# Two more units' convolution from TensorE to the channel-major jobs, with one product of most jobs moved from GpSimd to ScalarE

## Chip, cores, metric

The kernel runs on one core of a Trainium2 chip (trn2). The metric is device microseconds of a whole execution; a profile's span is 1.75 to 2.1 us shorter than the timed run. A ratio is the mean time of one kernel's fast runs over that of the kernel before in the same rounds, so it is not quite the ratio of the medians quoted beside it.

## The reference

```python
# causal convolution of 7 taps, one softmaxed set of taps per head (8 heads of 24 channels)
out = np.einsum('hk,bskhg->bshg', w, x_unf)        # x: 8 x 4096 tokens x 192 channels
x = out.reshape(32768, 192)
g = x @ w_gate                                     # 192 -> 1536
silu = g * (1.0 / (1.0 + np.exp(-g)))
return (silu * (x @ w_val) @ w_out)                # 1536 -> 192
```

## The kernel before

The tokens are cut into 16 units of 4 blocks of 512. A block goes through 12 steps, one for each chunk of 128 hidden features: a step multiplies the convolved block with a chunk of the gate and value weights on TensorE, takes silu on ScalarE (ACT) and the product h on VectorE (DVE). The down matmuls of finished chunks stand in four slots, after chunks 1, 4, 7 and 10.

The convolution runs ahead of its use in one of two ways. For a unit that is not "pooled" it is a band-matrix multiplication on TensorE (`conv_half`, twice a unit). For a pooled unit it is six jobs on channel-major tiles (channels on the partitions, tokens along the row), each of seven products with a per-channel tap: some on ACT, two on DVE, the rest on GpSimd (POOL), which also does the additions. Three jobs serve two blocks. GpSimd issues the "cast" that fetches a unit's tokens in fp16; SyncE's queue then issues the transposes to channel-major tiles and, once jobs are done, the "placement" of a block's results where the gate and value matmuls read them.

```python
    POOLED = (2, 4, 5, 6, 8, 9, 10, 12, 13, 14, 15)
    FIRST, ON_DVE, ON_ACT, ON_POOL = 0, (1, 2), (3,), (4, 5, 6)
    ...
        def add(part, k):                       # GpSimd: two 128x512 inputs
            total = job["total"]
            seq(nc.gpsimd.tensor_tensor(
                job["dst"] if k == K - 1 else total, total, part, op=ALU.add))

        def proceed():                          # once both DVE products are issued
            if job["dve"]:
                return
            while job["parts"]:
                add(*job["parts"].pop(0))       # what ScalarE has made
            if job["act"]:
                return
            for k in ON_POOL:                   # product into "piece", then the addition
                ...
        def dve_step(k):                        # total = x * tap + total, two 128x512 inputs
            seq(nc.vector.scalar_tensor_tensor(
                job["total"], shifted(k), job["tap"][:, k : k + 1], job["total"], ...))
    ...
    def pooled_work(n, j, busy):                # after each step's slot
        if not busy:
            ...
            if j in (1, 7, 10) and ready is not None:
                dve_steps.pop(0)[1]()
            if j in (1, 7, 10) and act_steps and (ready is None or ahead < ready + 3):
                act_steps.pop(0)[1]()
    ...
        elif j % 3 == 1 and n > 18:
            k = {1: 3, 4: 4, 7: 1, 10: 2}[j]
            slot(k, b - 1 if j < 7 else b, silu[n - 2], work)   # its first load waits for silu[n - 2]
```

Slot 4 (after chunk 4) ends with the output copies of the last block, half on ACT and half on DVE. Three PSUM buffers each serve gate and value, so the gate and value matmuls of step n wait until sig and h of step n - 3 are done.

## Time and profile before

| | before |
|---|---|
| time, median of 4 runs beside the changed kernel | 779.69 us (779.4 to 779.97) |
| span of the profile | 776.2 us |
| busy share PE, DVE, ACT, POOL | 99, 87, 75, 71% |
| a unit without disturbance | 46.92 us |
| extra over 46.92 us, units 1 to 14 | 4.84 us: convolution for units 3, 7, 11 4.32, two slips 0.52 |

The start of a unit is the start of its first gate weight load in the timeline; a unit's length is the distance to the next, and whatever is over 46.92 us is TensorE time lost or spent on convolution. The lost part is called a slip. Units 0 and 15 are left out: the first holds the loads, the last the end of the program.

The second part of the page cuts the span in 40 slices and gives busy tenths; POOL rests about once in four units, where the next unit's convolution is TensorE's:

```profile
POOL 9100798899999970299999995049999999996000
```

### The profile page before, as it was taken

The numbers are of one execution on the slowest core, as the hardware profiler recorded it, in microseconds if no ns is written. First come the engines' busy times: TensorE is split into PE (matmuls) and PEld (weight loads), VectorE is DVE, ScalarE is ACT, GpSimd is POOL, SyncE is SP. The second block draws the span as 40 slices with busy tenths as digits, with TensorE's granted clock in tenths as the row PEclk, the third lists the DMA queues.
The fourth block names the chain that finished last, engine by engine and source line by source line (L and its number), as shares of the span: only waits on it lengthen the run. The fifth ranks groups of instructions, "written<-read, shape, count | busy, mean of one in ns | idle before, by whom it ended". The sixth has DMA issues, their size and how long they took to land.

```text
span 776.2 us, 27852 instructions
## 1 busy us (share of the span) xinstructions
PE 770.1 (99%) x11307; PEld 627.2 (81%) x11307; DVE 675.0 (87%) x1018; ACT 584.6 (75%) x999; POOL 551.6 (71%) x523
## 2 busy tenths in 40 slices
PE   8999999999999999999999999999999999999998
PEld 5766776788888888678888888868888888888876
DVE  7686999999999977899999987799999999997775
ACT  6676887877877766878788776678788787876664
POOL 9100798899999970299999995049999999996000
PEclk9999999999999999999999999999999999999999
DMA  9959754944532295475363158557535254221211
GB/s 138 184 117 150 163 110 107 149 101 116 111 99 70 57 191 102 121 126 114 87 129 91 38 98 157 119 138 137 92 83 124 72 108 103 69 66 40 69 57 42
DMA packets 154470, 82.37 MB, mean 106 GB/s; under 512 B 98110, under 2 KB 153798, under 8 KB 153798
## 3 DMA queue, kind: packets, MB, share of 16 engines
q1 hardware_dynamic: 136422, 64.26, 37.6%
q0 software_dynamic: 17920, 16.34, 14.7%
q8 instruction: 88, 1.44, 0.8%
q14 instruction: 40, 0.33, 0.1%
HBM read 32.68 MB, written 38.34 MB: 91 GB/s over the span
## 4 chain that ended last, share of the span: by engine, by line
PE 99%; DVE 0%; ACT 0%; issue 0%
PE val L772 36%; PE acc L798 32%; PE gate L772 28%; PE cv L476 1%; PE warm L873 1%; PE turn L445 0%; PE cv L387 0%; PE acc L819 0%; DVE h L783 0%; ACT tme L405 0%; ACT wide L345 0%; ACT sig L781 0%; ACT o_sb L961 0%; DVE o_sb L857 0%; PE taps L332 0%
## 5 line engine op out<-in xcount | busy, mean ns | idle before, releaser
L781 ACT ACTIVATE sig<-gate 128x512 f16<-128x512 f32 x768 | 458.7, 597 | 175.0 <-PE gate L772 114.5
L783 DVE TENSOR_TENSOR h<-sig,val 128x512 f16<-128x512 f16 x768 | 502.6, 686 | 91.5 <-PE gate L772 64.1
L772 PEld LDWEIGHTS <-w 64*128 64x128 f16 x4608 | 359.6, 110 | 108.8 <-issue 1.5
L772 PE MATMUL gate<-pxc,w 64*128 64x512 f16 x1584 | 370.9, 376 | 0.0
L772 PE MATMUL val<-pxc,w 64*128 64x512 f16 x1584 | 370.7, 376 | 0.1
L798 PE MATMUL acc<-wo,h 64*128 64x192 f16 x6096 | 325.6, 243 | 0.0
L798 PEld LDWEIGHTS <-h 64*128 64x128 f16 x6096 | 299.8, 94 | 27.3 <-issue 1.9
L630 POOL TENSOR_TENSOR total<-total,piece 128x512 f32<-128x512 f32 x132 | 178.5, 1353 | 11.0
L772 PE MATMUL gate<-xc,w 64*128 64x512 f16 x720 | 169.6, 376 | 0.0
L772 PE MATMUL val<-xc,w 64*128 64x512 f16 x720 | 169.6, 376 | 0.1
L645 POOL TENSOR_SCALAR piece<-x,both_taps 128x512 f32<-128x512 f16 x198 | 165.2, 834 | 0.0
L655 DVE SCALAR_TENSOR_TENSOR total<-x,both_taps,total 128x512 f32<-128x512 f16 x132 | 138.8, 1052 | 0.0
L630 POOL TENSOR_TENSOR total<-total,part 128x512 f32<-128x512 f32 x66 | 89.9, 1362 | 52.2 <-DVE total L655 50.3
L630 POOL TENSOR_TENSOR pxc<-total,piece 128x512 f16<-128x512 f32 x44 | 58.9, 1340 | 3.7
L504 POOL COPY tm<-tm 128x1280 f16<-128x1280 f16 x4 | 5.0, 1251 | 65.7 <-DVE tm L493 65.7
L680 ACT ACTIVATE part<-x,both_taps 128x512 f32<-128x512 f16 x66 | 47.1, 714 | 0.0
L680 ACT ACTIVATE total<-x,both_taps 128x512 f32<-128x512 f16 x66 | 47.1, 713 | 0.0
L857 DVE COPY o_sb<-acc 128x384 f32<-128x384 f32 x63 | 34.7, 550 | 0.0
L630 POOL TENSOR_TENSOR y<-total,piece 128x512 f16<-128x512 f32 x22 | 29.2, 1329 | 1.8
L856 ACT COPY o_sb<-acc 128x384 f32<-128x384 f32 x63 | 30.3, 480 | 0.1
L98 POOL DMA_DIRECT2D x<-in_x_dram x10 | 8.7, 885 | 24.4 <-ACT sig L781 24.4
L493 ACT CAST tm<-cv 128x480 f16<-128x480 f32 x16 | 8.2, 562 | 5.6 <-PE cv L476 5.6
(67 smaller groups left out, 85.1 us busy)
## 6 DMA issues: line engine op xcount, KB each, us to landing
out_dram<-o_sb SPq DMA_DIRECT2D x63, 384.0 KB
pxc<-pxc SPq DMA_DIRECT2D x88, 64.0 KB
pxc<-y SPq DMA_DIRECT2D x88, 64.0 KB
xs<-in_x_dram POOLq DMA_DIRECT2D x7, 768.0 KB, 6.9
x<-in_x_dram POOLq DMA_DIRECT2D x10, 480.0 KB, 9.0
scr<-tm SPq DMA_DIRECT2D x28, 130.0 KB
xs<-in_x_dram POOLq DMA_DIRECT2D x4, 774.0 KB, 7.2
x<-x SPq DMA_DIRECT2D x6, 480.0 KB
```

The costliest lines, as they stand in the source:

```text
L98: nc.gpsimd.dma_start(out=t[p0 + i0 : p0 + i1, w0 - at : w1 - at, :], in_=bass.AP(tensor=x_flat.tensor, offset=(t0 + size * w0 - pad + i0) ...
L493: eng(tm[u][:, NG * r : NG * r + NG, 2 * grp * hp : 2 * grp * hp + 2 * grp].rearrange("p g (t e) -> p g t e", t=2), banks[r][:, 0 : 2 * w] ...
L630: nc.gpsimd.tensor_tensor(job["dst"] if k == K - 1 else total, total, part, op=ALU.add)
L645: nc.gpsimd.tensor_scalar(part, shifted(k), scalar1=job["tap"][:, k : k + 1], scalar2=1.0, op0=ALU.mult, op1=ALU.mult,)
L655: nc.vector.scalar_tensor_tensor(job["total"], shifted(k), job["tap"][:, k : k + 1], job["total"], op0=ALU.mult, op1=ALU.add,)
L680: nc.scalar.activation(part, shifted(k), AF.Copy, scale=job["tap"][:, k : k + 1])
L772: nc.tensor.matmul(o, w16[m][p0 : p0 + Q, k, e::E], xc[b][k][p0 : p0 + Q, 0:TB], start=(k == 0), stop=(k == SL - 1),)
L781: silu[n] = seq(nc.scalar.activation(sg, g, AF.Silu)).ins
L783: seq(nc.vector.tensor_tensor(hj, sg, v, op=ALU.mult))
L798: nc.tensor.matmul(acc[b][bank][:, s, :], hj[p0 : p0 + Q, ts(2 * bank + s, P)], wo16[p0 : p0 + Q, j, :], start=(not second and j == 0 and ...
L856: seq(nc.scalar.copy(o_sb[:, 0:2, :], acc[b][0]))
L857: seq(nc.vector.tensor_copy(o_sb[:, 2:4, :], acc[b][1]))
```

## The change

The intent: TensorE is the bound, so take the convolution of units 7 and 11 from it. All units but 1 and 3 are then channel-major (unit 0 has its own early path). GpSimd could not do three products in every job without rests (by the means of its rows before, three jobs take it 23.7 us, and the two blocks that they serve take TensorE 23.46), so two of three jobs give one to ScalarE, which gets an extra slot after chunk 4, ahead of the output copy.

```diff
-    POOLED = (2, 4, 5, 6, 8, 9, 10, 12, 13, 14, 15)
+    POOLED = (2, *range(4, NU))
...
-    FIRST, ON_DVE, ON_ACT, ON_POOL = 0, (1, 2), (3,), (4, 5, 6)
+    FIRST, ON_DVE = 0, (1, 2)
+    SHARES = ((3, 4), (5, 6)), ((3, 4), (5, 6)), ((3,), (4, 5, 6))
...
+        on_act, on_pool = SHARES[index % len(SHARES)]
...
+            if j == 4 and act_steps and act_steps[0][0] < (
+                dve_steps[0][0] if dve_steps else n_jobs[0]
+            ) + 3:
+                act_steps.pop(0)[1]()
             k = {1: 3, 4: 4, 7: 1, 10: 2}[j]
             slot(k, b - 1 if j < 7 else b, silu[n - 2], work)
```

Cut: the uses of `on_act` and `on_pool`, and a time table for unit 3 that is not reached, since unit 3 is not in the list.

More of the change, by code (lines that the diff above doesn't have):

```diff
@@ L620, in conv_job @@
         n_jobs[0] += 1
-        job = {"dve": len(ON_DVE), "act": len(ON_ACT), "parts": []}
+        on_act, on_pool = SHARES[index % len(SHARES)]
+        job = {"dve": len(ON_DVE), "act": len(on_act), "parts": []}
         at = XP - pad
@@ L641, in proceed @@
                 return
-            for k in ON_POOL:
+            for k in on_pool:
                 part = cpool.tile([P, TB], fp32, tag="piece", name="piece", bufs=2)
@@ L686, in act_step @@
                 proceed()
-        act_steps.extend((index, lambda k=k: act_step(k)) for k in (FIRST, *ON_ACT))
+        act_steps.extend((index, lambda k=k: act_step(k)) for k in (FIRST, *on_act))
     def place(u, i):
@@ L727, in planned @@
             times = (36, 36, 36, 38, 39, 39, 41, 41, 43, 43)
+        elif v == 3:
+            cast, jobs = 60, 56
+            times = range(66, 86, 2)
         else:
@@ L741, in pooled_work @@
         step_now[0] = n
-        if not busy:
+        if not busy and j != 4:
             ready = dve_steps[0][0] if dve_steps else None
```

## The prediction

> **What bounds the kernel now.** I read the page's busy shares and its chain first, then the windows view with one window per unit (a unit is 4 blocks of 512 tokens, 48 steps), then the timeline around single steps.
>
> ```profile
> PE 770.1 (99%) x11307; PEld 627.2 (81%) x11307; DVE 675.0 (87%) x1018; ACT 584.6 (75%) x999; POOL 551.6 (71%) x523
> ...
> PE val L772 36%; PE acc L798 32%; PE gate L772 28%; PE cv L476 1%; PE warm L873 1%; PE turn L445 0%; PE cv L387 0%; PE acc L819 0%; DVE h L783 0%; ACT tme L405 0%; ACT wide L345 0%; ACT sig L781 0%; ACT o_sb L961 0%; DVE o_sb L857 0%; PE taps L332 0%
> ```
>
> The chain is TensorE from end to end: gate, value and down matmuls, and 1% of convolution (cv). The unit starts for the windows are where the first gate weight load of each 48 steps begins in the timeline; shown are units 4, 5, 6 and 7 (columns: PE, PEld, DVE, ACT, POOL busy).
>
> ```profile
> 204.16:251.08 46.92, 46.92 (x676) 41.12 (x673) 44.24 (x65) 37.82 (x64) 45.50 (x41) 1.00 0.38 95
> 251.08:298.00 46.92, 46.92 (x676) 41.13 (x673) 39.23 (x58) 32.94 (x56) 34.87 (x33) 1.00 0.57 109
> 298.00:346.35 48.35, 48.35 (x740) 36.00 (x737) 41.23 (x63) 37.17 (x64) 19.19 (x19) 1.00 0.67 127
> 346.35:393.27 46.92, 46.92 (x676) 41.21 (x673) 44.30 (x65) 37.83 (x64) 45.48 (x42) 1.00 0.48 100
> ```
>
> Every undisturbed unit takes exactly 46.92 us, at full clock, so that is TensorE's own pace (11.73 us a block). Unit 6 takes 48.35 us because the convolution of unit 7 runs on TensorE inside it (64 more matmuls). The same 48.35 stands at unit 10 (for unit 11); unit 2 (for unit 3) has 48.38. Two odd slips remain, measured the same way: units 1 and 13 take 47.17 and 47.19, 0.25 and 0.27 over.
>
> [...] The timeline agrees: gate weight loads follow one another at 215 to 216 ns while gate and val halves run side by side, and down matmuls of 192 columns every 82 ns[...]. [...] The trace agrees for the VectorE product L655: alone it takes 0.745 us; started while a GpSimd instruction has the time r left, it takes about r + 0.55 (r = 0.48 gives 1.03, r = 0.96 gives 1.51, r = 1.21 gives 1.76). [...] the trace has 0.714 for exactly the product that is added, and that is used.
>
> **The change part by part.** I built both kernels and listed which slot issues each step of the convolution jobs.
>
> *Removed from TensorE.* Units 7 and 11 get 12 channel-major jobs on ACT, DVE and POOL instead. Units 6 and 10 lose 48.35 - 46.92 = 1.43 us each: **2.86 us**. All of it lies on the path, since TensorE never rests. That row of chain, 1%, is the whole stake; unit 3 and the early blocks keep theirs.
>
> *POOL.* The jobs' rows:
>
> ```profile
> L630 POOL TENSOR_TENSOR total<-total,piece 128x512 f32<-128x512 f32 x132 | 178.5, 1353 | 11.0
> ...
> L645 POOL TENSOR_SCALAR piece<-x,both_taps 128x512 f32<-128x512 f16 x198 | 165.2, 834 | 0.0
> L655 DVE SCALAR_TENSOR_TENSOR total<-x,both_taps,total 128x512 f32<-128x512 f16 x132 | 138.8, 1052 | 0.0
> ...
> L680 ACT ACTIVATE part<-x,both_taps 128x512 f32<-128x512 f16 x66 | 47.1, 714 | 0.0
> ```
>
> A job before is 4 additions and 3 products: 4 x 1.353 + 3 x 0.834 = 7.91 us; three jobs in two blocks are 23.7 us against 2 x 11.73 = 23.46 of TensorE. So POOL could not hold that for long, which is why every fourth unit went to TensorE. After, two of three jobs lose one product (4 additions still): 7.91 + 2 x 7.08 = 22.07 us, 94% of 23.46. GpSimd keeps up, idle some 1.4 us in two blocks; one cast issue per unit (0.56 us) fits in that.
>
> *DVE.* Twelve products a unit in twelve slots, as in units 4 and 7 now: 44.3 of 46.92 us busy, unchanged in a full unit, but now in all of units 3 to 14 rather than with rests.
>
> *ACT.* Four more products a unit. Back to back it starts the next instruction 0.103 us before the last ends (median of sig to product), so 4 x (0.714 - 0.103) = 2.44 us on 37.82: 40.3 of 46.92, 86%. The average is harmless; the place is not. One block of unit 4:
>
> ```profile
> 232.83 0.48 ACT L856 COPY o_sb<-acc 128x384 f32<-128x384 f32 x1
> ...
> 233.40 1.89 ACT L781 ACTIVATE sig<-gate 128x512 f16<-128x512 f32 x3
> ...
> 234.28 1.21 PEld L798 LDWEIGHTS <-h 64*128 64x128 f16 x23
> ```
>
> The listing of waits has the first down weight load (at 234.28) wait for the sig of chunk 5, which ends at 234.00 now. With a product after sig of chunk 4 (end 232.86): product 232.76 to 233.47, output copy 233.37 to 233.85, sig of chunk 5 from 233.75 to 234.34. The one time that this load did wait in the trace (at 27.51 us) it started 0.05 us after the sig's end; so 234.39 instead of 234.28. But the load stands 0.214 us ahead of its matmul (234.50) and takes 0.094, so the matmul can still start at about 234.49. I estimate no loss in most blocks, with almost nothing to spare: 0 to 0.05 us in each of some 52 blocks, **0 to 2.6 us**; I take 0.3.
>
> *Lateness on DVE.* h of chunks 5 to 7 comes 0.35 us later. Their room, from h's end to the first weight load of the matmuls that reuse the bank, is 0.69, 0.56, 0.56 now; it stays positive.
>
> **Sum.** 779.74 - 2.86 + 0.3 = 777.2. The two slips could go (-0.5) or others come.
>
> **The rivals.** (a) *ACT blocks the down matmuls.* If copy or sig start without the 0.103 overlap after a product, sig of chunk 5 ends 0.1 to 0.2 us later, and each block loses that: 52 x 0.15 = 8 us, time about 785. For it: the margin is 0.01 us by my sum. Against it: the overlap is 0.10 wherever two ACT instructions have nothing to wait for (also CAST after CAST).
>
> (b) *Lock step of GpSimd and VectorE.* The tight place is after chunk 1: h of chunk 2 to 4 have 0.19, 0.06, 0.06 us of room, and the product of that slot stands before them. Products up to 1.505 us there cost nothing in the trace; in unit 13 one of 1.79 cost 0.27:
>
> ```profile
> 632.24 1.79 DVE L655 SCALAR_TENSOR_TENSOR total<-x,both_taps,total 128x512 f32<-128x512 f16 x1
> 633.96 1.87 DVE L783 TENSOR_TENSOR h<-sig,val 128x512 f16<-128x512 f16 x3
> ```
>
> It began 0.03 us after a GpSimd addition did. Before, GpSimd drifts against TensorE, so this is chance (2 of 45). After, GpSimd rests once in two blocks, at the job whose second product stands after chunk 7, and then always starts from the same point: the phase repeats in every period. Laying out the operations from that rest (additions 1.27, products 0.69, plus 0.44 when locked out), I find at the two slots after chunk 1 a rest of about 0.3 and 0.5 to 0.93 us of an addition, that is products of 0.9 and 1.1 to 1.48 us: no loss. If my phase is off by some 0.2 us in the bad direction, one slot in two blocks loses up to 0.27: some 24 x 0.27 = 6.5 us, time about 783.
>
> (c) *GpSimd falls behind anyway* (lockouts make it longer than 23.46): then jobs end late. They are placed 16 steps ahead of use and finish tens of steps earlier, so a lag of a few us is absorbed; only ACT's waits for part buffers could then bite. POOL at 94% speaks against it; it would give 780 to 790.
>
> (d) *The gain is hidden:* impossible to see how, as TensorE has no idle time in units 6 and 10.
>
> **Range and chances.** The floor is 779.74 - 2.86 - 0.5 = 776.4; run scatter is 0.3 on either side. (a) and (b) have no floor above it and I give them together one in five, mostly at partial size. So 776.0 to 780.2. Two per cent is 15.6 us: a gain of that is beyond the stake, a loss needs (a) and (b) in full together.
>
> **What would show it.** Right: the windows of units 6 and 10 at 46.92; no wait of down weight loads on ACT of more than 0.1 us each in the list of waits; POOL waiting for the DVE product about once in two blocks; product L655 after chunk 1 under 1.5 us; ACT's sig of chunk 5 ending about 0.34 us later. Wrong: units of 47.1 to 47.6 us all along (a: the gap stands ahead of the down loads after chunk 7; b: ahead of the gate or val matmul of chunk 5), or POOL without rests (c).

Cut from the prediction, and marked, are figures and a mechanism that no trace of this case shows; what the traces show beside them stays (where it says that a trace agrees, it is with a passage that is cut). Its sum came to 779.74 - 2.86 + 0.3 = 777.2 us, with the added ScalarE product at the traced 0.714 us. That a unit of 46.92 us could not be made shorter was the estimate; the trace shows TensorE busy for all 46.92.

## The result

The changed kernel takes 777.82 us (777.55 to 777.89, 4 runs), 1.87 us less; ratio 0.9975, 95% interval 0.9958 to 0.9993. The result is correct. The gain is a quarter of a per cent, but the interval lies below 1. The spans of the two profiles (776.2 and 776.0) show less than that, because the profiled execution of before was a fast one (778.31 us); the reason is in unit 0 and comes with the last experiment.

The page's busy shares and its chain, after:

```profile
PE 767.9 (99%) x11179; PEld 599.6 (77%) x11179; DVE 687.4 (89%) x1034; ACT 607.6 (78%) x1067; POOL 597.8 (77%) x551
...
PE val L777 41%; PE acc L803 33%; PE gate L777 22%; DMA xe<-in_x_dram 1%; POOL w L168 0%; DVE h L788 0%; POOL xe L98 0%; PE cv L476 0%; PE acc L824 0%; PE cv L387 0%; PE turn L445 0%; ACT sig L786 0%; DVE o_sb L862 0%; ACT o_sb L970 0%; POOL jn L192 0%
```

TensorE has 128 matmuls fewer and is still the chain (97% after 99%; most of the rest is loads at the start). DVE h, which stood in it before too, now comes ahead of cv, both under 0.5%. The slices of POOL show its long rests gone:

```profile
POOL 9100697799999999999999999999999999992000
```

The windows view of units 4, 6, 7 and 10 after (columns as in the prediction: PE, PEld, DVE, ACT, POOL busy):

```profile
204.92:251.84 46.92, 46.92 (x675) 38.46 (x673) 43.19 (x65) 38.62 (x68) 44.05 (x39) 1.00 0.45 100
298.76:345.71 46.95, 46.95 (x675) 38.40 (x673) 44.10 (x64) 38.64 (x68) 44.06 (x40) 1.00 0.48 100
345.71:392.95 47.24, 47.12 (x676) 38.32 (x673) 44.83 (x66) 38.83 (x68) 44.35 (x40) 1.00 0.46 103
487.18:534.40 47.22, 47.11 (x676) 38.28 (x674) 44.82 (x66) 38.84 (x68) 44.33 (x40) 1.00 0.51 107
```

Unit 6 went from 48.35 to 46.95, unit 10 from 48.35 to 47.22 only, and unit 7 from 46.92 up to 47.24. Of units 3 to 13 nine are longer than 46.92, by 0.03 to 0.32 us: 1.75 us in all. The account for units 1 to 14:

| | before | after |
|---|---|---|
| convolution in unit 2 (for unit 3) | 1.46 | 1.28 |
| convolution in units 6 and 10 | 2.86 | 0 |
| slips | 0.25 (unit 1), 0.27 (unit 13) | 1.75 (units 3 and 6 to 13) |
| sum, rounded as the traces give it | 4.84 | 3.02 |

The difference is 1.82 us. So the removal paid in full, and 1.2 us net of it was lost to slips. That it nearly equals the 1.87 of the timed runs is in part chance: the end of the program takes 0.55 us more after the change (see before_again), and a timed run exceeds its span by 1.75 us there against 2.0 to 2.1 before. Neither was foreseen.

One slip in unit 7, from the timeline of the changed kernel (start, duration):

```profile
347.90 0.69 POOL L647 TENSOR_SCALAR piece<-x,both_taps 128x512 f32<-128x512 f16 x1
...
348.65 1.84 DVE L657 SCALAR_TENSOR_TENSOR total<-x,both_taps,total 128x512 f32<-128x512 f16 x1
348.67 1.27 POOL L632 TENSOR_TENSOR total<-total,piece 128x512 f32<-128x512 f32 x1
...
349.92 1.14 POOL L647 TENSOR_SCALAR piece<-x,both_taps 128x512 f32<-128x512 f16 x1
...
350.42 1.87 DVE L788 TENSOR_TENSOR h<-sig,val 128x512 f16<-128x512 f16 x3
...
351.15 1.44 PEld L777 LDWEIGHTS <-w 64*128 64x128 f16 x15 [0.29 <-issue]
```

The VectorE product after chunk 1 starts within 0.02 us of a GpSimd addition, which takes 1.27 us. The product, though its recorded start is the earlier one, is over at 350.49, 0.55 us after the addition, instead of 0.75 us after its own start. The h of chunks 2 to 4 come late, and TensorE stands still for 0.29 us ahead of the matmuls of chunk 5 that reuse their banks. This is the prediction's rival (b).

The ScalarE side in the changed kernel, unit 5 (timeline):

```profile
268.70 0.71 ACT L682 ACTIVATE total<-x,both_taps 128x512 f32<-128x512 f16 x1
...
269.32 0.47 ACT L861 COPY o_sb<-acc 128x384 f32<-128x384 f32 x1
...
269.68 1.58 ACT L786 ACTIVATE sig<-gate 128x512 f16<-128x512 f32 x3
...
270.34 0.72 PEld L803 LDWEIGHTS <-h 64*128 64x128 f16 x14
```

Product, copy and the next sig stand end to end, as laid out. The sig of chunk 5 ends at 270.29, the first down load starts 0.05 us later, and its matmul another 0.117 us on, where it would have been anyway. In blocks without a slip TensorE loses nothing here.

The groups of the changed kernel that answer to those of before:

```profile
L657 DVE SCALAR_TENSOR_TENSOR total<-x,both_taps,total 128x512 f32<-128x512 f16 x156 | 166.3, 1066 | 0.0
L647 POOL TENSOR_SCALAR piece<-x,both_taps 128x512 f32<-128x512 f16 x182 | 154.4, 848 | 0.0
...
L682 ACT ACTIVATE part<-x,both_taps 128x512 f32<-128x512 f16 x130 | 93.3, 718 | 0.0
```

GpSimd's products went from 198 to 182 although there are 12 jobs more; ACT's went from 66 to 130. The DVE product is a little slower on average (1.066 after 1.052), which says nothing of where it is slow.

### The profile page after: what moved, and what is told of

Read it like the earlier page. It is cut to its first block, busy times and chain, and to the rows that moved or that the text cites. A ratio compares the mean times of both kernels' runs of the same rounds, so it can differ in the third digit from the quotient of the medians.

```text
span 776.0 us, 27834 instructions
## 1 busy us (share of the span) xinstructions
PE 767.9 (99%) x11179; PEld 599.6 (77%) x11179; DVE 687.4 (89%) x1034; ACT 607.6 (78%) x1067; POOL 597.8 (77%) x551
## 4 chain that ended last, share of the span: by engine, by line
PE 97%; POOL 1%; DMA 1%; DVE 1%; issue 0%; ACT 0%; DVEq 0%; POOLq 0%
PE val L777 41%; PE acc L803 33%; PE gate L777 22%; DMA xe<-in_x_dram 1%; POOL w L168 0%; DVE h L788 0%; POOL xe L98 0%; PE cv L476 0%; PE acc L824 0%; PE cv L387 0%; PE turn L445 0%; ACT sig L786 0%; DVE o_sb L862 0%; ACT o_sb L970 0%; POOL jn L192 0%
## 5 line engine op out<-in xcount | busy, mean ns | idle before, releaser
L777 PEld LDWEIGHTS <-w 64*128 64x128 f16 x4608 | 338.9, 110 | 135.2 <-issue 1.9
L777 PE MATMUL gate<-pxc,w 64*128 64x512 f16 x1872 | 438.7, 376 | 0.0
L777 PE MATMUL val<-pxc,w 64*128 64x512 f16 x1872 | 437.6, 376 | 0.5
L632 POOL TENSOR_TENSOR total<-total,part 128x512 f32<-128x512 f32 x130 | 173.0, 1330 | 45.6 <-DVE total L657 21.8
L657 DVE SCALAR_TENSOR_TENSOR total<-x,both_taps,total 128x512 f32<-128x512 f16 x156 | 166.3, 1066 | 0.0
L632 POOL TENSOR_TENSOR total<-total,piece 128x512 f32<-128x512 f32 x104 | 141.6, 1362 | 8.7
L777 PE MATMUL gate<-xc,w 64*128 64x512 f16 x432 | 102.1, 377 | 0.0
L777 PE MATMUL val<-xc,w 64*128 64x512 f16 x432 | 101.9, 376 | 0.1
L682 ACT ACTIVATE part<-x,both_taps 128x512 f32<-128x512 f16 x130 | 93.3, 718 | 0.0
L632 POOL TENSOR_TENSOR pxc<-total,piece 128x512 f16<-128x512 f32 x52 | 70.3, 1353 | 4.3
```

Of the source, the lines that this page charges most:

```text
L632: nc.gpsimd.tensor_tensor(job["dst"] if k == K - 1 else total, total, part, op=ALU.add)
L657: nc.vector.scalar_tensor_tensor(job["total"], shifted(k), job["tap"][:, k : k + 1], job["total"], op0=ALU.mult, op1=ALU.add,)
L682: nc.scalar.activation(part, shifted(k), AF.Copy, scale=job["tap"][:, k : k + 1])
L777: nc.tensor.matmul(o, w16[m][p0 : p0 + Q, k, e::E], xc[b][k][p0 : p0 + Q, 0:TB], start=(k == 0), stop=(k == SL - 1),)
```

## The experiments

All kernels are the changed kernel with a small edit, unless said otherwise. "Extra" is the sum over 46.92 us in units 1 to 14, from the one profile of each (where the slips of a kernel scatter, this is one draw: after_again was profiled in its slowest execution, 778.77 us, the other four took 776.58 to 777.06); in brackets the part that is not convolution on TensorE. The kernel before took 779.25 to 779.58 us (medians) in these rounds.

| run | time us | ratio | extra |
|---|---|---|---|
| before_again | 779.68 | 1.0001 | 4.83 (0.52) |
| after_again | 776.93 | 0.9973 | 3.53 (2.25) |
| split_only | 780.50 | 1.0014 | 5.71 (1.53) |
| old_split | 796.01 | 1.0209 | 20.46 (19.0) |
| no_port (wrong result) | 775.12 | 0.9949 | 1.28 (0) |
| act_dose | 782.78 | 1.0046 | 7.97 (6.7) |
| cast_in_rest | 785.68 | 1.0076 | 8.89 (7.6) |
| cast_other | 782.47 | 1.0042 | 6.94 (5.7) |
| pool_extra | 780.36 | 1.0017 | 4.53 (3.2) |
| heavy_second | 778.46 | 0.9990 | 4.16 (2.9) |
| heavy_first | 779.62 | 1.0007 | 5.02 (3.7) |
| unit3 | 817.94 | 1.0488 | 47.75 (47.7) |

My theory after the result (theory A) was that the slips come from which GpSimd instruction happens to run when the DVE product starts: a product that starts inside one takes what is left of it plus about 0.55 us (in the traces of before and after; called blocked below). Why the two engines do so is not shown here. The rival (theory B) was plain load: DVE, at 43 to 45 of 46.92 us a unit, and GpSimd have too little room.

### The cost of the blocking by itself: no_port

Condensed from the edit:

```diff
-                nc.gpsimd.tensor_tensor(job["dst"] if k == K - 1 else total, total, part, op=ALU.add)
+            if part is not None:        # one element each, to keep the waits
+                seq(nc.gpsimd.tensor_copy(tiny[:, 0:1], total[:, 0:1]))
+                seq(nc.gpsimd.tensor_copy(tiny[:, 1:2], part[:, 0:1]))
+            count(); count()            # iota into a scratch tile, no input tile
+            if k == K - 1: seq(nc.gpsimd.memset(job["dst"], 0.0))
...
-                    nc.gpsimd.tensor_scalar(part, shifted(k), ...)
+                count()
```

> WRONG RESULT ON PURPOSE. The changed kernel, with each GpSimd addition replaced by two iota instructions and each GpSimd product by one (they write a scratch tile and read no SBUF, about 0.55 us each by the two iotas of the trace), one-element copies to keep the waits for VectorE and ScalarE, and a memset of the result. GpSimd stays about as busy, everything else is the same. Theory A [...]: every product takes 0.74 to 0.80 us, no slips in units 2 to 14 beyond the convolution in unit 2, extra over 46.92 us about 1.3 us in place of 3.0 and 3.5, time about 1.8 us below the changed kernel. Theory B (VectorE has too much to do, or ScalarE's new place): the slips stay.

Every unit from 3 to 14 took 46.92 us exactly; the extra is the 1.28 us of convolution and nothing else. The DVE products' group of this run:

```profile
L659 DVE SCALAR_TENSOR_TENSOR total<-x,both_taps,total 128x512 f32<-128x512 f16 x156 | 116.4, 746 | 0.0
```

All 156 took 0.744 to 0.75 us, 51 of them started in the middle of a GpSimd instruction that had over 0.25 us to go, which was none of the one-element copies (0.185 us each). GpSimd was less busy than planned (541.8 against 597.8 us), so load is not held exactly; but the 51 overlapping products show that overlap alone cost nothing beside what GpSimd ran here, mostly iotas (806, 0.555 us each) and memsets (0.524 us), which have no input tile. DVE's instructions and ACT's extra slot are those of the changed kernel, so neither is the cause by itself: the blocking beside GpSimd's additions and products is, and it is what the change loses, 1.75 us in its profile. What in those instructions blocks was not shown. One thing this run can't separate: a blocked product counts as busy, so DVE's busy time fell too, to 41.16 us a unit. That the place of the blocking decides, and not only its sum, rests on the runs with moved work below. The time agrees: by the ratios to the kernel before (0.9949 against 0.9973 and 0.9975) no_port is 1.9 to 2.0 us under the changed kernel.

### Is the place of the slips fixed: after_again

> The changed kernel once more, beside the others of this call, with a second profile. If the places of the slips are set by the fixed order and not by chance, the profile shows them again at chunk 1 of the first block of units 6 to 13 (0.03 to 0.31 us each, some 1.5 us in all); time about 777.8. If they come by chance, another pattern.

The edit is none. Half a miss: units 6 and 9 to 12 slip in the same place as in the first profile (after chunk 1 of the first block), but in units 7, 8 and 13 the product came just ahead of the addition there (0.746 us) and the slip moved to the third block, with 2.25 us of slips against 1.75. Unit 7 in this profile:

```profile
349.20 0.75 DVE L657 SCALAR_TENSOR_TENSOR total<-x,both_taps,total 128x512 f32<-128x512 f16 x1
349.26 1.82 POOL L632 TENSOR_TENSOR total<-total,piece 128x512 f32<-128x512 f32 x1
```

Here the addition starts 0.059 us after the product and is the one that is blocked; in the first profile it started 0.018 us after it and won. All kept traces together draw the line sharply: all 24 additions that started up to 0.037 us after a product (with no cast under way) blocked it (the product took 1.82 to 1.86 us), and all that started 0.046 to 0.082 us after it were blocked themselves, the product taking under 0.75. A shift of 0.03 to 0.04 us, which the order of the instructions does not fix, so moves the slip.

### Moving the cast: cast_in_rest and cast_other

Once a unit GpSimd also issues a cast (0.55 us). In the changed kernel it stands between the first and second job of a period (three jobs, two blocks), and after it the third job starts 0.5 us later than in the next period, which is the one with the 1.84 us product. I took the cast for the culprit.

```diff
-            cast, jobs = s0 - 115, s0 - 89
+            cast, jobs = s0 - 127, s0 - 89      # cast_in_rest; cast_other: s0 - 124
```

> The changed kernel, with the cast issue of each unit 12 steps earlier (step 17 of 24 in place of step 5), where GpSimd rests 0.69 us ahead of the third job; the issue takes 0.55. Theory A (phase): the cast pushes the second job 0.57 us back, its last addition then meets the VectorE product after chunk 7, the third job starts 0.5 us late, and 16 us on the product after chunk 1 of the unit's first block starts with a GpSimd addition and takes 1.5 to 1.84 us. With the cast in the rest the phase is the same in every two blocks: products after chunk 1 of 1.0 to 1.35 us, all of units 5 to 14 at 46.92 us (1.5 us of slips gone), time about 776.3. Theory B (VectorE and GpSimd are simply near full, so slips come whatever the place): slips of the same sum, about 777.8.

> Control to cast_in_rest: the cast is 9 steps earlier than in the changed kernel, but ahead of the first job of a period and not in the rest. Theory A: it again delays the second job by about 0.55 us, so the third job is late once a unit and the slips stay, 0 to 0.31 us a unit, sum 1 to 2 us, time about 777.5 to 778. If the earlier cast as such (its DMA traffic) were what helps, this run should be as fast as cast_in_rest. Theory B: 777.8.

Both expectations for cast_in_rest failed. With the cast in the rest the phase did become the same every two blocks, and this phase is a bad one. From the timeline of VectorE, unit 7:

```profile
352.77 1.03 DVE L657 SCALAR_TENSOR_TENSOR total<-x,both_taps,total 128x512 f32<-128x512 f16 x1
...
364.50 1.74 DVE L657 SCALAR_TENSOR_TENSOR total<-x,both_taps,total 128x512 f32<-128x512 f16 x1
```

The product after chunk 1 is 1.03 us in one block and 1.74 in the next, throughout: the second addition of the second job starts 0.08 us ahead of it. Each costs 0.2 us, twice a unit, 4.7 us in all. So the cast in the changed kernel is not the culprit. By pushing the second job it takes this product away from the bad place, at the price of a bad one once a unit elsewhere. In cast_other the slips stayed as theory A said (2.3 us, where 1 to 2 were expected; the expected time was missed by the stall that follows).

The rest of the loss in both, 2.9 and 3.4 us, is one stall in unit 2 that I had not expected. SyncE's queue of cast_in_rest, and then of the changed kernel:

```profile
134.24 9.88 SPq L512 DMA_DIRECT2D scr<-tm  x8
```

```profile
134.42 5.13 SPq L512 DMA_DIRECT2D scr<-tm  x8
```

The eight stores of unit 3's convolution took 9.88 us to issue in place of 5.13; the placement of unit 2's last block stands behind them in the same queue, and TensorE waited for it. The cast of unit 5 was issued at 133.29 us, just ahead of these stores; that its traffic slowed them is argued from the times, not shown apart.

### More GpSimd work: pool_extra

```diff
+        if ls == 42 and 240 < n < 650:
+            seq(nc.gpsimd.tensor_copy(gb, ga))   # 128x960 scratch, ahead of the third job
         pooled_work(n, j, work is not None)
```

Cut: the two scratch tiles and the memset of one.

> The changed kernel with MORE GpSimd work: one copy of some 1 us on two scratch tiles, once a unit, just ahead of the third job whose phase causes the slip. Theory A: the third job starts about 0.3 us later, the product after chunk 1 then starts while a GpSimd product (0.69 us) is in its last part and takes about 0.8 us in place of 1.84: the slips of units 6 to 13 go (below 0.05 us each), time about 776.5, with more work. Theory B (load): more GpSimd work makes it the same or worse, 777.8 to 779.

The product that had taken 1.84 us in unit 7 took 0.74, as theory A said, and units 5, 8, 9 and 14 had no extra at all, which load alone would not give. But others grew to 1.7 to 2.4 us, and units 6 and 7 lost 0.7 and 0.8. The two longest there, 2.07 and 2.36 us, started while GpSimd was issuing the cast, and the addition behind the cast, 0.23 and 0.52 us later, still came first; in cast_in_rest ten products that started during a cast, with the next addition 0.89 us off, took 0.74. Why is open. The expected time was missed, and the runs scatter (778.93 to 782.19). Shifting the phase once a unit shifts every later meeting too.

### Which job is the long one: heavy_second, heavy_first

```diff
-    SHARES = ((3, 4), (5, 6)), ((3, 4), (5, 6)), ((3,), (4, 5, 6))
+    SHARES = ((3, 4), (5, 6)), ((3,), (4, 5, 6)), ((3, 4), (5, 6))      # heavy_second
+    SHARES = ((3,), (4, 5, 6)), ((3, 4), (5, 6)), ((3, 4), (5, 6))      # heavy_first
```

> The changed kernel, but the job that leaves three products to GpSimd (7.9 us) is the second of each three and not the third. The third job becomes ready 6 steps (5.9 us) ahead of the next one, the second 9 steps (8.8 us), so the long job no longer runs 2 us into the next. Theory A (the slip is set by which GpSimd instruction is running when the product after chunk 1 starts): by the rule that a product takes the rest of the running instruction plus 0.55 us, the products after chunk 1 come to 0.8 to 1.2 us, no slips in units 5 to 13, time about 776.3. Theory B (load alone): the load is the same, so 777.8.

> The third place for the long GpSimd job: the first of each three. Load is the same as in the changed kernel and in heavy_second (sum of slips 1.7 to 2.9 us in units 3 to 14 there). If the sum is set by chance of phase, this one gives another pattern of the same order, 776.3 to 779.5. If some place of the long job is free of slips, 776.3.

In heavy_second the products after chunk 1 did become short (mean 1.01 us, all but one under 1.48). The slips did not go: products after chunks 7 and 10 now took up to 1.85 us, and TensorE lost 0.1 to 0.3 us at the third block of each unit. I had looked at one tight place only. heavy_first has two places a unit, 0.12 and 0.31 us, 3.7 us in all. With nearly the same load (pool_extra has some more), six placements gave slips of 1.75 to 4.7 us; the changed kernel's, 1.75 and 2.25 in its two profiles, are the smallest of those that I tried.

### ScalarE's margin: act_dose

```diff
                 act_steps.pop(0)[1]()
+                seq(nc.scalar.copy(late, fill))      # 128x128, useless; its tile is cut
```

> The changed kernel with a useless 128x128 ScalarE copy behind each added product, ahead of the output copy of chunk 4 (52 times, about 0.3 us long, 0.2 net). Claim: the added product of 0.71 us costs nothing because the first down load after chunk 7 stands 0.117 us ahead of its matmul and could come closer by only about 0.036 us. So the margin is used up: each of 52 blocks should lose about 0.2 - 0.036 = 0.16 us, 8 us in all, time about 786, with the gap ahead of the down loads after chunk 7. If there is still room on ScalarE there, the time stays at 777.8.

The copy took 0.286 us, and the sig of chunk 5 starts and ends 0.20 us later. In 41 of the 52 blocks TensorE then lost 0.10 us ahead of the down loads after chunk 7, and the list of waits names it:

```profile
PEld L804 <- ACT sig L787: 13.6, 41, 0.5
```

The load still starts 0.051 us after the sig's end, but its lead to the matmul shrank from 0.117 to 0.004 us. So the added product is indeed free, with a margin of about 0.20 - 0.10 = 0.10 us, nearly three times the 0.036 that I had expected (an estimate whose working is not on record; 0.117 less 0.081, the median lead of a down load over its matmul in the changed kernel's trace, gives it). In place of the expected 8 us, some 4.1 came from this; the rest of the 6.7 is mostly slips, since the phase moved here as well (in units 4 to 13 a slip of 0.2 us in the second block; after it the down loads of that block were not late).

### The parts alone: old_split and split_only

old_split has the new unit list, the old split (one product on ACT) and no extra slot; split_only the old unit list with everything else new.

```diff
-    SHARES = ((3, 4), (5, 6)), ((3, 4), (5, 6)), ((3,), (4, 5, 6))
+    SHARES = (((3,), (4, 5, 6)),)                                   # old_split
...
-            if j == 4 and act_steps and act_steps[0][0] < (
+            if False and act_steps and act_steps[0][0] < (          # old_split
```

```diff
-    POOLED = (2, *range(4, NU))
+    POOLED = (2, 4, 5, 6, 8, 9, 10, 12, 13, 14, 15)                 # split_only
```

> Only the unit list of the change: units 7 and 11 go to the channel-major jobs, but every job keeps one product on ScalarE after the first and three on GpSimd, and ScalarE has no extra slot. GpSimd then needs three times 7.9 us and the gaps between dependent operations, about 24.5 us, in 23.46: it should fall 1 to 1.3 us behind every two blocks. Expected: no rests on GpSimd, a lag that grows to over 20 us by unit 14; the data are still in time for long, so the cost is only the chance slips and some stall at the end: 777 to 785. If the new split was not needed, about 777.

> Only the new split and the extra ScalarE slot, units 7 and 11 stay on TensorE. TensorE keeps the 1.43 us in units 6 and 10, so nothing is gained: 779.2 to 780.5, with units 6 and 10 at 48.35 us again. If the split itself made something faster, below 779.

old_split fell behind as reckoned: the time from a job's second DVE product to its last addition grows from 8 us to 14 to 16 in three pooled units (as before the change, where the rest at unit 7 resets it) and on to 18 to 20; in the changed kernel it stays at 7 to 9.5. But I had held the lag to be harmless until over 20 us, and of the 19 us that were lost, 18 fall in units 7 to 14. GpSimd's queue also holds the casts, so these come late (up to 9 us later in a unit than in the changed kernel), and SyncE's transposes wait for them in order, ahead of the placements. The waits of the DMA queue, old_split and then the changed kernel (us in total, times, longest):

```profile
SPq L605 <- DMA xs<-in_x_dram: 173.7, 11, 19.4
```

```profile
SPq L605 <- DMA xs<-in_x_dram: 107.1, 11, 10.9
```

split_only brought nothing, at 780.50 us (95% interval of the ratio 1.0000 to 1.0028): units 6 and 10 are 48.37 us again, and the split alone makes slips (1.5 us against 0.5). So the unit list is the whole gain, and the split is what makes it possible.

### One step further: unit3

```diff
-    POOLED = (2, *range(4, NU))
+    POOLED = tuple(range(2, NU))
...
-            if n < max(done + (12 if u == 2 else 18), ustep * u + NCH * i - 16):
+            if n < max(done + (12 if u < 4 else 18), ustep * u + NCH * i - 16):
```

> The change carried one step further: unit 3 channel-major too (its cast and jobs in the place that the changed kernel has ready for it, its blocks placed 12 steps after the last product). TensorE saves the two convolution halves in unit 2, 2 x 0.64 = 1.28 us. Expected 776.5 if unit 3's blocks are placed in time, with slips in unit 2 or 3 as elsewhere; some us above 777.8 if TensorE waits for the first placements of unit 3.

Far from it: 817.94 us. TensorE loses 8.4 us at the start of unit 2 (in the three steps around it, against no_port), and 0.5 to 4.9 us at the start of each of units 4 to 13. For unit 2 the trace shows what is late: the placement of its first block, which SyncE's queue issues from 96.12 us on in the changed kernel, is issued only from 113.90 us on, behind the transposes of unit 3 in the same queue:

```profile
112.12 1.27 SPq L605 DMA_TRANSPOSE x<-xs  x1
113.90 0.46 SPq L706 DMA_DIRECT2D pxc<-pxc  x1
```

The later units I did not take apart; what is late there is open.

### Startup: before_again

> The kernel before, unchanged, for a second profile of it. In the profile of the changed kernel TensorE waits 0.8 us in unit 0 (ahead of a down matmul that the listing of waits puts behind the load of the output weights), in that of before it does not, which hides most of the gain in the two spans (776.2 and 776.0). If that wait is chance of the first loads, this profile shows one like it (0.2 to 1.5 us more than 3.52 in that group of three chunks, as in all the other runs); if the change brings it, 3.52 again. Units 1 to 14 should repeat: 1.43 to 1.46 in units 2, 6, 10 and slips of 0.25 and 0.27 in units 1 and 13, extra 4.8 us in all. Time equal to before.

The kernel before once more. Units 1 to 14 repeat to 0.03 us (4.83 extra). In unit 0 the group of three chunks that took 3.52 us in its first profile took 4.83 this time; the changed kernel has 4.32 and 4.41, and no other profile is under 4.00. So that wait varies with the first loads, not with the change, and the span of before was a lucky one. The timed runs carry the comparison. From the last group of three chunks to the end of the program the changed kernel takes 9.9 us in place of 9.35. The steps and the last output copies stand at the same distances; the 0.55 us lie behind the last output's issue, among the closing semaphores and drains, and stay unexplained.

## Why the prediction was right, and where not

- **The predicted range, 776.0 to 780.2,** held 777.82, and the repeat of 776.93. The expected gain was 2.5 us and 1.87 came.
- **Removed from TensorE, 2.86 us, all on the path: right.** no_port has units 6 and 10 at 46.92, and split_only puts 48.37 back. The gain was not hidden in those units (d).
- **POOL keeps up: right; its rest was mis-sized.** Predicted idle some 1.4 us in two blocks, measured 0.69 as a rest. The working took busy times alone. Between two dependent GpSimd operations (product to its addition, addition to addition) the timeline has a gap of 0.08 us, nine in three jobs, 0.72 us.
- **ACT, 0 to 2.6 us, taken 0.3: the mechanism was right and the cost is zero.** The sig of chunk 5 ends 0.33 us later (0.34 predicted), the load starts 0.05 us after it as laid out, and the margin is 0.10 us where the sum gave 0.01. Rival (a) did not come, though by the letter its sign did: in eight blocks of units 1 to 3 the list has the load wait 0.20 us for that sig, over the 0.1 named, at no cost to TensorE. ACT is busy 38.6 us in a full unit and not 40.3: the added products are there, but the sigs behind them now overlap one another (three in 1.58 us in unit 5 above, in 1.89 in the prediction's block). On DVE the room of chunks 5 to 7 fell to 0.36, 0.27 and 0.32 us and stayed positive, as predicted.
- **Rival (b) came, and "I find at the two slots after chunk 1 ... no loss" is the step that failed.** The mechanism (remaining time plus 0.55 us) held: in the changed kernel all 106 products that met over 0.3 us of a GpSimd instruction took 0.535 to 0.56 us more than what was left of it. It has exceptions in other runs: 0.72 for one product in before and for some in heavy_second and old_split, and the products that start during a cast. The phase did not hold: from unit 3 on 13 of 46 products after chunk 1 took over 1.5 us, up to 1.85, where all should have stayed under it. As I read the timeline (no run isolates it), the missing 0.08 us gaps let GpSimd run into the DVE product after chunk 7, from where the third job starts later than laid out. It came once a unit, not in every two blocks, since the cast shifts the phase once a unit; with the cast out of the way it did come once in every two blocks, 0.2 us each. That the cast softened it was luck: the prediction counted the cast as load only.
- **The sum was near because two errors cancelled in part.** Slips were 1.75 where the sum had none (its 0.3 was for ACT, which cost nothing); against that the two old slips went (0.52, expected only as a chance) and unit 2's convolution cost 0.18 less, which I had not foreseen. split_only has that 0.18 too and old_split has not, so it comes with the new split; why is open.
- **Rival (c)**: not in the changed kernel, and much worse than "780 to 790" in old_split: the lag is carried into the DMA queue by the casts.

What carries the result is the blocking: 1.84 us in place of 0.75 where a product meets a fresh addition, and at most 0.75 in no_port. It goes both ways: a GpSimd product that starts inside a DVE product takes 1.14 us in place of 0.69 (unit 7 above). By the trace's start times the earlier one goes first only to some 0.04 us (the 0.037 and 0.046 under after_again). The 0.08 us gap between dependent GpSimd operations stands against an overlap of 0.02 to 0.03 where the next one does not depend. The reserve on the ScalarE side is the lead of the first down load over its matmul: 0.214 us before the change, of which 0.117 was enough; one of 0.004 went with a loss of 0.10 us (act_dose).

## What to carry to other kernels

Here, where the bound engine was truly full, moving work off it paid its full duration (2.86 us of 2.86), but the engines that took it over needed room in every place and not only on average: look for the step with the smallest slack and ask what can stretch the instruction in front of it. Two engines that block each other (1.84 us in place of 0.75) made this kernel's time depend on phase, so that a move of the cast to a rest brought more slips (4.7 us against 1.75), and less GpSimd work, in split_only, came with more slips (1.53 us against 0.52); count the gaps between dependent operations before trusting a laid-out phase, and try several orders. GpSimd's queue, which carries both work and transfer issues in order, passed its lag on to everything behind those transfers (old_split: 173.7 us of SyncE's waits for the casts in place of 107.1).
